# Four small edits to a tuned attention-plus-MLP kernel: epsilon inside bn_stats, a last tile in three pieces, a short final wait, and 1/den spread by DMAs

## The chip, the cores and the metric

The kernel runs on one core of one Trainium2 chip. The metric is the device time of one execution in microseconds (us). Runs are fast: the granted TensorE clock (the share of full speed that the profile shows as allowed) was 0.99 to 1.00.

Engine names as in the profile: PE is TensorE's matmuls, PEld its weight loads, DVE is VectorE, ACT is ScalarE, POOL is GpSimd, SP is SyncE, SPq its DMA queue. The pitch of a row of instructions is the time from one start to the next. A DMA lands when its semaphore reports it done.

## The reference

A layernorm without gain, then two branches on it, added to x. S = 2048 tokens, D = 640, F = 1536, 32 heads of 20, bf16.

```python
xn = (x - mean(x)) / sqrt(var(x) + 1e-5)
q, k, v = split_heads(xn @ wqkv)
phi = lambda t: where(t > 0, t + 1, exp(t)) + 1e-6
kv  = einsum("bhsd,bhse->bhde", phi(k), v)
z   = einsum("bhsd->bhd", phi(k))
den = einsum("bhqd,bhd->bhq", phi(q), z)[..., None] + 1e-6
a   = merge_heads(einsum("bhqd,bhde->bhqe", phi(q), kv) / den) @ wo
b   = gelu_tanh(xn @ w1 + b1) @ w2 + b2
return x + a + b
```

## The kernel before

The tokens are 16 tiles of 128 and 4 chunks of 512. The order on PE is: warm-up matmuls, transposes of the normalised tiles and the first MLP matmul (HG), the k projection, the sums over tokens, the q projection in chunks with the small matmuls that build one 640x640 matrix `Msb` of the attention between them, and last the output tiles. An output tile is 17 accumulating steps in PSUM, the memory that the matmuls write to: 12 of HG with W2, and 5 of PQ with Msb, where PQ is phi(q) times 1/den. Its eviction is the DVE instruction that adds x and writes the sum to SBUF, from where it is stored.

A small planner in the kernel records which instruction reads and writes which resource, and puts a semaphore wait wherever one depends on another, on the same engine too (PE excepted).

The layernorm statistics: `bn_stats` leaves sums over half a tile, `bn_aggr` makes mean and variance of the two halves, and `rstd` is the variance plus epsilon to the power of -1/2. Both halves of a tile's `stats` are one resource. `g` is POOL, `v` is DVE.

```python
def ln_half(t, h):
    s = t % 4
    Pl.ins(v, lambda e: e.bn_stats(stats[:, s, 6*h:6*h+6], x_in[:, t, h*HW:(h+1)*HW]),
           reads=[r_x[t]], writes=[r_stats[s]])

def ln_aggr(t):
    s = t % 4
    Pl.ins(v, lambda e: e.bn_aggr(aggr[:, s, :], stats[:, s, :]), reads=[r_stats[s]], writes=[r_aggr[s]])
    Pl.ins(g, lambda e: e.tensor_single_scalar(veps[:, s:s+1], aggr[:, s, 1:2], EPS, ALU.add), ...)
    Pl.ins(g, lambda e: e.tensor_tensor(out=rstd[:, s:s+1], in0=veps[:, s:s+1], in1=mhalf[:], op=ALU.pow), ...)

def ln_next(t):            # the order on DVE from tile 2 on
    if t + 1 < NT: ln_half(t + 1, 0); ln_half(t + 1, 1)
    ln_norm(t)
    if t + 1 < NT: ln_aggr(t + 1)
```

1/den of a chunk lies on 32 partitions, one for each head. A matmul with a 0/1 matrix `E4` spreads it to 128, ACT copies it to SBUF, DVE multiplies five tiles of PQ.

```python
def rden_step(c, b):
    # ... cut: cc is the columns of chunk c, rs a buffer in ek
    Pl.ins("tensor", lambda e: e.matmul(bank(b), E4[:, c, :], rden[:], start=True, stop=True), ...)
    Pl.ins("scalar", lambda e: e.activation(rs, bank(b), ACT.Copy), ...)
    for j in range(DT):
        Pl.ins(v, lambda e, j=j: e.tensor_tensor(out=PQ[:, j, cc], in0=PQ[:, j, cc], in1=rs, op=ALU.mult), ...)

def x_again(c):            # x is loaded once more for the residual, over the space of xnT
    # ... cut
    Pl.ins("sync", lambda e: e.dma_start(x_res[:, c*CH:(c+1)*CH, :], src), writes=[r_xr[c]] + r_xnT, dma=True)
```

The last tile is two halves of 320 columns, each with its own eviction and store, and at the end SP waits for every DMA it ever issued:

```python
def out_last(t):
    # ... cut
    for h in range(2):
        # ... cut
        Pl.ins("tensor", [mm(b, t, i, h) for i in range(JT + DT)], ...)
        Pl.ins(v, lambda e, h=h, hs=hs: e.tensor_tensor(out=out_sb[:, h, 0:HW], in0=bank(b+h, 0, HW), in1=x_res[:, t, hs], op=ALU.add), ...)
        Pl.ins("sync", lambda e, h=h, hs=hs: e.dma_start(ov[t*P:(t+1)*P, hs], out_sb[:, h, 0:HW]), ...)
# ... cut ...
for (waits, fns, ev, dma) in list(Pl.records["sync"]):
    if dma and ev is not None:
        Pl.wait_event("sync", ev)
```

Of the kernel before, what the change touches and what calls it, by code (L numbers as in the profile page):

```python
# [5 lines left out]
ALU = AluOpType  # L6
ACT = mybir.ActivationFunctionType
P = 128
FP32 = mybir.dt.float32
# [103 lines left out]
def bass_parallel_sum__linear_attn_block__dense_activation_gelu__prompt_kernel(  # L113
    nc: bass.Bass, A_x, A_wqkv, A_wo, B_x, B_w1, B_b1, B_w2, B_b2, out):
    Batch, S, D = A_x.shape
# [4 lines left out]
    CW = CH * P  # L120
    NC = NT // CH
    DT = D // P
    JT = F // P
    H = 32
    DH = D // H
    HW = D // 2
    assert DH == 4 * DT
    EPS = 1e-5

    Pl = Planner(nc)  # L130
    R_ = Pl.res
# [5 lines left out]
    with contextlib.ExitStack() as es:  # L137
        sb = lambda *a, **k: es.enter_context(nc.sbuf_tensor(*a, **k))
# [7 lines left out]
        x_res = xnTf[:].rearrange("p (t d) -> p t d", t=NT)  # L146
        PQ = sb("PQ", [P, DT, S], BF16)
        HG = sb("HG", [P, JT, S], BF16)
# [5 lines left out]
        W2 = sb("W2", [P, JT, D], BF16)  # L154
        Wo = sb("Wo", [P, DT, D], BF16)
        Mf = sb("Msb", [P, DT * D], BF16)
        Msb = Mf[:].rearrange("p (k d) -> p k d", k=DT)
# [11 lines left out]
        warm = sb("warm", [P, 512], BF16)  # L169
        stats = sb("stats", [P, 4, 12], FP32)  # L170
        aggr = sb("aggr", [P, 4, 2], FP32)
        veps = sb("veps", [P, 4], FP32)
        rstd = sb("rstd", [P, 4], FP32)
        mhalf = sb("mhalf", [P, 1], FP32)
        z_sb = sb("z_sb", [P, DT], FP32)
        ek = sb("ek", [P, 3, D], BF16)
        den_sb = sb("den_sb", [P, CW], FP32)
        rden = sb("rden", [P, CW], BF16)
        out_sb = sb("out_sb", [P, 2, D], BF16)

        ps = es.enter_context(nc.psum_tensor("ps", [P, 8 * 512], FP32))
        B_ = [R_("bank%d" % i) for i in range(8)]
        ring = [0]

        def take(n):
            b = ring[0]
            if n == 2 and b % 2:
                b += 1
            b %= 8
            ring[0] = (b + n) % 8  # L190
            return b

        def bank(b, lo=0, hi=512):
            return ps[:, b * 512 + lo: b * 512 + hi]
# [4 lines left out]
        def halves(ap):  # L199
            return ap.rearrange("p (a n) -> p a n", a=2)  # L200

        r_x = [R_("x%d" % t) for t in range(NT)]
        r_xr = [R_("xr%d" % c) for c in range(NC)]
        r_xb = [R_("xb%d" % t) for t in range(NT)]
        r_xn = [R_("xn%d" % t) for t in range(NT)]
        r_xnT = [R_("xnT%d" % t) for t in range(NT)]
# [2 lines left out]
        r_Wq, r_Wk, r_Wv, r_W2, r_Wo = R_("Wq"), R_("Wk"), R_("Wv"), R_("W2"), R_("Wo")  # L209
        r_b1tmp, r_b1c, r_b2 = R_("b1tmp"), R_("b1c"), R_("b2")  # L210
        r_ident, r_small, r_masks, r_bmask, r_E4, r_warm = R_("ident"), R_("small"), R_("masks"), R_("bmask"), R_("E4"), R_("warm")
        r_stats = [R_("stats%d" % i) for i in range(4)]
        r_aggr = [R_("aggr%d" % i) for i in range(4)]
        r_veps = [R_("veps%d" % i) for i in range(4)]
        r_rstd = [R_("rstd%d" % i) for i in range(4)]
        r_ek = [R_("ek%d" % i) for i in range(3)]
        r_PK = [R_("PK%d" % t) for t in range(NT)]
        r_PQ = [[R_("PQ%d_%d" % (c, j)) for j in range(DT)] for c in range(NC)]
# [5 lines left out]
        r_den, r_rden = R_("den"), R_("rden")  # L224
        r_out = [R_("out0"), R_("out1")]

        xv = A_x.rearrange("b s d -> (b s) d")
        ov = out.rearrange("b s d -> (b s) d")
# [25 lines left out]
        for c in range(2, NC):  # L254
# [9 lines left out]
        g = "gpsimd"  # L264
        v = "vector"
# [7 lines left out]
               reads=[r_ident], writes=[r_ident])  # L273
# [37 lines left out]
        def ln_half(t, h):  # L311
            s = t % 4
            Pl.ins(v, lambda e: e.bn_stats(stats[:, s, 6 * h:6 * h + 6], x_in[:, t, h * HW:(h + 1) * HW]),  # L313
                   reads=[r_x[t]], writes=[r_stats[s]])

        def ln_aggr(t):
            s = t % 4
            Pl.ins(v, lambda e: e.bn_aggr(aggr[:, s, :], stats[:, s, :]),
                   reads=[r_stats[s]], writes=[r_aggr[s]])
            Pl.ins(g, lambda e: e.tensor_single_scalar(veps[:, s:s + 1], aggr[:, s, 1:2], EPS, ALU.add),  # L320
                   reads=[r_aggr[s]], writes=[r_veps[s]])
            Pl.ins(g, lambda e: e.tensor_tensor(out=rstd[:, s:s + 1], in0=veps[:, s:s + 1],
                                                in1=mhalf[:], op=ALU.pow),
                   reads=[r_veps[s], r_small], writes=[r_rstd[s]])

        def ln_stats(t):
            ln_half(t, 0)
# [54 lines left out]
        def h_first(jbs):  # L382
# [7 lines left out]
            for jb, b in zip(jbs, bs):  # L390
# [6 lines left out]
               reads=[r_warm], writes=[r_b1c])  # L397
# [47 lines left out]
        for t in range(TD, NT):  # L445
            if t > TD:
                ln_next(t)
            Pl.ins("sync", lambda e, t=t: e.dma_start_transpose(xnT[:, :, t * P:(t + 1) * P], xn_tm[:, t, :]),
                   reads=[r_xn[t]], writes=[r_xnT[t]], dma=True)
# [22 lines left out]
        for t in range(NT):  # L472
            b = take(2)
            fns = []
# [10 lines left out]
        for f in range(DT):  # L485
            b = take(2)
            for t in range(NT):
# [3 lines left out]
                    reads=[r_xn[t], r_PK[t]], writes=B_[b:b + 2])  # L491
            Pl.ins("scalar", lambda e, b=b, f=f: e.activation(halves(GTb[:, f, :]), pair(b), ACT.Copy),
                   reads=B_[b:b + 2], writes=[r_GT[f]] + r_W1)

        Pl.ins(v, lambda e: e.tensor_tensor(out=zsum, in0=PK[:, 0, :], in1=PK[:, 1, :], op=ALU.add),
               reads=[r_PK[0], r_PK[1]], writes=[r_zsum])
        for t in range(2, NT):
            Pl.ins(v, lambda e, t=t: e.tensor_tensor(out=zsum, in0=zsum, in1=PK[:, t, :], op=ALU.add),  # L498
                   reads=[r_PK[t], r_zsum], writes=[r_zsum])
# [3 lines left out]
               reads=[r_zsum, r_zhl], writes=[r_zhl])  # L503
# [50 lines left out]
        def den_step():  # L554
# [8 lines left out]

            return b

        def rden_step(c, b):
            cc = slice(c * CW, (c + 1) * CW)
            s = c % 3
            rs = ek[:, s, 0:CW]
            Pl.ins("tensor", lambda e: e.matmul(bank(b), E4[:, c, :], rden[:], start=True, stop=True),  # L570
                   reads=[r_E4, r_rden], writes=[B_[b]])
            Pl.ins("scalar", lambda e: e.activation(rs, bank(b), ACT.Copy), reads=[B_[b]], writes=[r_ek[s]])  # L572
            for j in range(DT):
                Pl.ins(v, lambda e, j=j: e.tensor_tensor(out=PQ[:, j, cc], in0=PQ[:, j, cc], in1=rs, op=ALU.mult),  # L574
                       reads=[r_ek[s], r_PQ[c][j]], writes=[r_PQ[c][j]])

        def x_again(c):
            src = xv[c * CW:(c + 1) * CW, :].rearrange("(t p) d -> p t d", p=P)
            Pl.ins("sync", lambda e: e.dma_start(x_res[:, c * CH:(c + 1) * CH, :], src),
                   writes=[r_xr[c]] + r_xnT, dma=True)  # L580

        def xb(t):
            Pl.ins(v, lambda e: e.tensor_tensor(out=x_res[:, t, :], in0=x_res[:, t, :], in1=b2bc[:], op=ALU.add),
# [9 lines left out]
        for c in range(NC):  # L593
            x_again(c)


        def mm(b, t, i, h):
            tok = slice(t * P, (t + 1) * P)
            l, r = ((HG[:, i, tok], W2[:, i, :]) if i < JT else (PQ[:, i - JT, tok], Msb[:, i - JT, :]))
            return lambda e: e.matmul(bank(b + h, 0, HW), l, r[:, h * HW:(h + 1) * HW],  # L600
                                      start=(i == 0), stop=(i == JT + DT - 1))

        def mm_reads(t, i):
            return [r_HG[t][i], r_W2] if i < JT else [r_PQ[t // CH][i - JT], r_M[i - JT]]

        def out_w2(t, lo=0, hi=JT, b=None):
            b = take(2) if b is None else b
            for i in range(lo, hi):
                Pl.ins("tensor", [mm(b, t, i, 0), mm(b, t, i, 1)], reads=mm_reads(t, i), writes=B_[b:b + 2],
                       mark=(i == JT - 1))  # L610
            return b

        def out_fin(t, b):
            s = t % 2
            for i in range(JT, JT + DT):
                Pl.ins("tensor", [mm(b, t, i, 0), mm(b, t, i, 1)], reads=mm_reads(t, i), writes=B_[b:b + 2],
                       mark=(i == JT + DT - 1))
            xb(t)
            Pl.ins(v, lambda e: e.tensor_tensor(out=halves(out_sb[:, s, :]), in0=pair(b),  # L619
                                                in1=halves(x_res[:, t, :]), op=ALU.add),  # L620
                   reads=B_[b:b + 2] + [r_xb[t]], writes=[r_out[s]])
            Pl.ins("sync", lambda e: e.dma_start(ov[t * P:(t + 1) * P, :], out_sb[:, s, :]),
                   reads=[r_out[s]], dma=True)

        def out_last(t):
            b = take(2)
            xb(t)
            for h in range(2):
                hs = slice(h * HW, (h + 1) * HW)
                Pl.ins("tensor", [mm(b, t, i, h) for i in range(JT + DT)],  # L630
                       reads=[r for i in range(JT + DT) for r in mm_reads(t, i)], writes=[B_[b + h]])
                Pl.ins(v, lambda e, h=h, hs=hs: e.tensor_tensor(
                    out=out_sb[:, h, 0:HW], in0=bank(b + h, 0, HW), in1=x_res[:, t, hs], op=ALU.add),
                    reads=[B_[b + h], r_xb[t]], writes=[r_out[h]])
                Pl.ins("sync", lambda e, h=h, hs=hs: e.dma_start(ov[t * P:(t + 1) * P, hs], out_sb[:, h, 0:HW]),
                       reads=[r_out[h]], dma=True)

        bs = [out_w2(0)]
        db = den_step()
        bs += [out_w2(1), out_w2(2, 0, JT // 2)]  # L640
        rden_step(0, db)
        out_w2(2, JT // 2, JT, bs[2])
        for t in range(3):
            out_fin(t, bs[t])
        for t in range(3, NT - 1):
            b = out_w2(t)
            if t in (3, 6, 10):
                rden_step({3: 1, 6: 2, 10: 3}[t], take(1))
            out_fin(t, b)
        out_last(NT - 1)  # L650

        for (waits, fns, ev, dma) in list(Pl.records["sync"]):
            if dma and ev is not None:
                Pl.wait_event("sync", ev)

        with contextlib.ExitStack() as ses:
            for e_ in ENGINES:
# [33 lines left out]
```

## Time and profile before

| | before |
|---|---|
| time, median of 3 runs | 211.89 us (211.79 to 212.27) |
| span of the profiled run | 210.7 us (its time was 212.41 us, above all of the others) |
| PE busy | 98% |
| PE without work | to 5.8 us (but for warm-up), 0.5 us before 8.48, 0.2 us before 12.32, about 1 us in 122 to 126, after 207.8 |

From the page of the kernel before: the span, the busy time of each engine (us, share, instructions), and the chain of work that ended last, by engine.

```profile
span 210.7 us, 3883 instructions
PE 205.5 (98%) x1585; PEld 140.1 (67%) x1585; DVE 110.5 (52%) x226; ACT 76.8 (36%) x145; POOL 20.5 (10%) x61
...
PE 86%; DVE 7%; DMA 4%; SPq 1%; issue 1%; DVEq 0%
```

Only what shortens PE's own work, its few pauses, or the tail can move the time. The start, from the timelines of PE and of DVE: start, duration, line, operation, tiles and count, and in brackets the idle time before and what ended it.

```profile
8.48 3.78 PE L356 MATMUL ps<-xnT,W 128*128 128x128 bf16 x55 [0.35 <-DMA W<-in_B_w_dram]
12.32 0.45 PE L340 MATMUL ps<-ident,xn_tm 128*128 128x128 bf16 x5
```

```profile
10.88 1.02 DVE L313 BATCH_NORM_STATS2 stats<-xPK 128x6 f32<-128x320 bf16 x2 [0.69 <-DMA xPK<-in_A_x_dram]
11.82 0.43 DVE L333 TENSOR_SCALAR xn_tm<-xPK,aggr,rstd 128x640 bf16<-128x640 bf16 x1
```

PE waits first for a piece of W1 (it is loaded in four, 0 to 3) that lands at 8.43 us, then at 12.32 us for the transposes of tile 2. Tile 2 is normalised at 11.82 us, because DVE runs the two `bn_stats` of tile 3 first, and tile 3 lands at 10.86 us.

One of the three matmuls that the change takes out, in the timeline of PE. The next group starts 0.21 us later with nothing idle between, though the profile gives the matmul itself 0.38 us (matmuls overlap):

```profile
146.96 3.42 PE L600 MATMUL ps<-W,HG 128*128 128x320 bf16 x24
150.22 0.38 PE L570 MATMUL ps<-rden,E 128*128 128x512 bf16 x1
150.43 1.52 PE L600 MATMUL ps<-Msb,PQ 128*128 128x320 bf16 x10
```

The tail, from the timeline of all engines: the last eviction, and the two last stores merged into one row (the second is issued at 208.4 us). Then, from the answers about single lines of the program, the times from issue to landing of these two stores, and SP's final waits with their durations in ns and the start of the first and of the last.

```profile
206.50 2.19 SPq L635 DMA_DIRECT2D out_dram<-out_sb  x2
...
207.84 0.49 DVE L632 TENSOR_TENSOR out_sb<-ps,xnT 128x320 bf16<-128x320 f32 x1 [1.37 <-PE ps L600]
```

```profile
DMA to landing us min/median/max: 1.6/1.6/1.6
...
L108 SPq EVENT_SEMAPHORE  x17: 28/28/28, 208.7 to 210.2; - x17
```

The last store lands at 209.94 us, but the list of waits runs on to 210.2 us and the span ends at 210.66. Each instruction of the list carries two waits.

### The profile page before, as it was taken

Reading aid. Unit: us, or ns where it says so; the run is one execution under the profiler, and the core shown is the slowest. Engines: PE = TensorE matmul, PEld = TensorE weight load, DVE = VectorE, ACT = ScalarE, POOL = GpSimd, SP = SyncE. Lnnn points to the kernel's source line nnn. Section 1 sums busy time; section 2 is a strip of 40 time slices with the busy share of each in tenths; the row PEclk is TensorE's granted clock in tenths of the full one; section 3 lists DMA queues with packets and bytes.
Section 4 is the critical chain, followed back from the end, with each engine's and each line's share of the span. In section 5 each row is a group of like instructions: output and inputs, shape, how many; then the busy total and the mean of one; then the engine's idle time right before and its main releaser. Section 6 shows DMA issues by size and latency. Waiting matters only on the chain.

```text
span 210.7 us, 3883 instructions
## 1 busy us (share of the span) xinstructions
PE 205.5 (98%) x1585; PEld 140.1 (67%) x1585; DVE 110.5 (52%) x226; ACT 76.8 (36%) x145; POOL 20.5 (10%) x61
## 2 busy tenths in 40 slices
PE   7999999999999999999999999999999999999994
PEld 2689987444457777777666555677777777777772
DVE  4689981000008888999078866468451522263221
ACT  2579887666676554111253575110100100100000
POOL 2244557700000000000000000000000000000000
PEclk9999999999999999999999999999999999999999
DMA  5994758999000000000000000355411010001011
GB/s 165 340 349 99 101 111 101 347 321 346 10 0 0 0 3 0 0 3 0 0 0 3 0 5 0 124 138 170 163 35 54 9 65 31 31 31 34 31 62 33
DMA packets 21787, 17.46 MB, mean 83 GB/s; under 512 B 8713, under 2 KB 21769, under 8 KB 21769
## 3 DMA queue, kind: packets, MB, share of 16 engines
q1 hardware_dynamic: 21088, 16.72, 27.6%
q10 hardware_dynamic: 680, 0.49, 0.9%
q8 instruction: 12, 0.20, 0.4%
q14 instruction: 7, 0.05, 0.1%
HBM read 12.62 MB, written 2.62 MB: 72 GB/s over the span
## 4 chain that ended last, share of the span: by engine, by line
PE 86%; DVE 7%; DMA 4%; SPq 1%; issue 1%; DVEq 0%
PE ps L600 35%; PE ps L356 23%; PE ps L477 10%; PE ps L488 10%; PE ps L510 5%; DMA xPK<-in_A_x_dram 4%; DVE PQ L467 3%; DVE ek L465 1%; DVE W L534 1%; SPq L232 1%; PE ps L530 1%; PE ps L546 1%; DVE ZB L524 1%; PE ps L556 1%; DVE stats L313 0%
## 5 line engine op out<-in xcount | busy, mean ns | idle before, releaser
L600 PE MATMUL ps<-W,HG 128*128 128x320 bf16 x384 | 54.9, 299 | 0.0
L356 PE MATMUL ps<-xnT,W 128*128 128x128 bf16 (+2 forms) x435 | 52.0, 282 | 0.4 <-DMA W<-in_B_w_dram 0.4
L600 PEld LDWEIGHTS ps<-W,HG 128*128 128x128 bf16 x384 | 37.5, 98 | 15.2 <-issue 0.4
L356 PEld LDWEIGHTS ps<-xnT,W 128*128 128x128 bf16 x435 | 35.5, 98 | 16.1 <-DMA W<-in_B_w_dram 0.5
L360 ACT ACTIVATE HG<-ps,b1c 128x128 bf16<-128x128 f32 (+2 forms) x87 | 40.0, 492 | 13.2 <-PE ps L356 11.1
L465 DVE TENSOR_SCALAR ek<-ek 128x512 bf16<-128x512 bf16 (+1 forms) x36 | 10.9, 304 | 40.2 <-ACT ek L464 39.1
L464 ACT ACTIVATE ek<-ps 128x512 bf16<-128x512 f32 (+1 forms) x36 | 23.2, 644 | 20.4 <-PE ps L510 11.2
L619 DVE TENSOR_TENSOR out_sb<-ps,xnT 128x640 bf16<-128x640 f32 x15 | 12.4, 825 | 29.3 <-PE ps L600 26.2
L600 PE MATMUL ps<-Msb,PQ 128*128 128x320 bf16 x160 | 24.2, 299 | 0.0
L510 PE MATMUL ps<-xnT,Wqkv 128*128 128x512 bf16 x100 | 22.1, 379 | 0.0
L477 PE MATMUL ps<-Wqkv,xnT 128*128 128x320 bf16 x160 | 21.9, 299 | 0.0
L488 PE MATMUL ps<-xPK,xn_tm 128*128 128x320 bf16 x160 | 21.9, 299 | 0.0
L572 ACT ACTIVATE ek<-ps 128x512 bf16<-128x512 f32 x4 | 2.4, 597 | 49.2 <-PE ps L570 49.2
L600 PEld LDWEIGHTS ps<-Msb,PQ 128*128 128x128 bf16 x160 | 15.6, 98 | 6.3
L477 PEld LDWEIGHTS ps<-Wqkv,xnT 128*128 128x128 bf16 x160 | 15.7, 98 | 6.2
L488 PEld LDWEIGHTS ps<-xPK,xn_tm 128*128 128x128 bf16 x160 | 15.7, 98 | 6.1
L510 PEld LDWEIGHTS ps<-xnT,Wqkv 128*128 128x128 bf16 x100 | 11.6, 118 | 9.5 <-issue 0.2
L313 DVE BATCH_NORM_STATS2 stats<-xPK 128x6 f32<-128x320 bf16 x32 | 15.2, 475 | 3.5 <-DMA xPK<-in_A_x_dram 2.9
L467 DVE SCALAR_TENSOR_TENSOR PQ<-ps,ek 128x512 bf16<-128x512 f32 x20 | 13.8, 692 | 2.1
L467 DVE SCALAR_TENSOR_TENSOR xPK<-ps,ek 128x640 bf16<-128x640 f32 x16 | 13.2, 825 | 1.7
L498 DVE TENSOR_TENSOR Msb<-Msb,xPK 128x640 f32<-128x640 f32 x14 | 11.6, 825 | 0.5
L574 DVE TENSOR_TENSOR PQ<-PQ,ek 128x512 bf16<-128x512 bf16 x20 | 7.1, 419 | 9.0 <-ACT ek L572 9.0
(64 smaller groups left out, 89.3 us busy)
## 6 DMA issues: line engine op xcount, KB each, us to landing
xnT<-in_A_x_dram SPq DMA_DIRECT2D x4, 640.0 KB, 4.1
Wqkv<-in_A_wqkv_dram SPq DMA_DIRECT2D x3, 800.0 KB, 6.9
out_dram<-out_sb SPq DMA_DIRECT2D x15, 160.0 KB, 1.8
W<-in_B_w_dram SPq DMA_DIRECT2D x1, 1920.0 KB, 15.3
W<-in_B_w_dram SPq DMA_DIRECT2D x3, 480.0 KB, 7.6
xPK<-in_A_x_dram SPq DMA_DIRECT2D x2, 640.0 KB, 9.3
Wo<-in_A_wo_dram SPq DMA_DIRECT2D x1, 800.0 KB, 10.5
xPK<-in_A_x_dram SPq DMA_DIRECT2D x4, 160.0 KB, 4.5
```

Source lines behind the costliest of these rows:

```text
L313: Pl.ins(v, lambda e: e.bn_stats(stats[:, s, 6 * h:6 * h + 6], x_in[:, t, h * HW:(h + 1) * HW]), reads=[r_x[t]], writes=[r_stats[s]])
L356: Pl.ins("tensor", [(lambda e, k=k: e.matmul(bank(b, 0, w), W1[:, k, jb * P:(jb + 1) * P], xnT[:, k, tok], start=(k == 0), stop=(k == DT - ...
L360: Pl.ins("scalar", lambda e: e.activation(HG[:, jb, tok], bank(b, 0, w), ACT.Gelu_apprx_tanh, bias=b1c[:, jb:jb + 1]), reads=[B_[b], r_b1c ...
L464: Pl.ins("scalar", lambda e: e.activation(e2, src, ACT.Exp), reads=br, writes=[r_ek[s]])
L465: Pl.ins(v, lambda e: e.tensor_scalar(et, et, 1.0, 1e-6, ALU.min, ALU.add), reads=[r_ek[s]], writes=[r_ek[s]])
L467: Pl.ins(v, lambda e: e.scalar_tensor_tensor(out=d2, in0=src, scalar=0.0, in1=e2, op0=ALU.max, op1=ALU.add), reads=br + [r_ek[s]], writes= ...
L477: fns.append(lambda e, k=k, h=h, b=b, t=t: e.matmul(bank(b + h, 0, HW), xnT[:, k, t * P:(t + 1) * P], Wqkv[:, k, D + h * HW:D + (h + 1) * ...
L488: Pl.ins("tensor", [(lambda e, t=t, h=h, b=b, f=f: e.matmul(bank(b + h, 0, HW), xn_tm[:, t, f * P:(f + 1) * P], PK[:, t, h * HW:(h + 1) * ...
L498: Pl.ins(v, lambda e, t=t: e.tensor_tensor(out=zsum, in0=zsum, in1=PK[:, t, :], op=ALU.add), reads=[r_PK[t], r_zsum], writes=[r_zsum])
L510: Pl.ins("tensor", [(lambda e, k=k, j=j, b=b: e.matmul(bank(b), Wqkv[:, k, j:D:DT], xnT[:, k, cc], start=(k == 0), stop=(k == DT - 1))) fo ...
L600: return lambda e: e.matmul(bank(b + h, 0, HW), l, r[:, h * HW:(h + 1) * HW], start=(i == 0), stop=(i == JT + DT - 1))
L619: Pl.ins(v, lambda e: e.tensor_tensor(out=halves(out_sb[:, s, :]), in0=pair(b), in1=halves(x_res[:, t, :]), op=ALU.add), reads=B_[b:b + 2] ...
```

## The change

Four parts, meant to take work off PE and off the two ends of the kernel: (1) 1/den of chunks 1 to 3 is spread by four small DMAs each instead of a matmul and an ACT copy, and the reloads of x no longer wait for each other; (2) the last tile is three pieces of 320, 192 and 128 columns; (3) SP's final wait is for the last 3 stores; (4) epsilon, times D, is added to a sum that `bn_stats` leaves, while DVE does the second half, instead of to the variance afterwards, and for this the halves of `stats` became two resources. The diff, cut:

```diff
 def ln_half(t, h):
-           reads=[r_x[t]], writes=[r_stats[s]])
+           reads=[r_x[t]], writes=[r_stats[s][h]])
+    if h == 0:
+        Pl.ins(g, lambda e: e.tensor_single_scalar(stats[:, s, 2:3], stats[:, s, 2:3], D * EPS, ALU.add),
+               reads=[r_stats[s][0]], writes=[r_stats[s][0]])
 def ln_aggr(t):
-           reads=[r_stats[s]], writes=[r_aggr[s]])
-    Pl.ins(g, lambda e: e.tensor_single_scalar(veps[:, s:s + 1], aggr[:, s, 1:2], EPS, ALU.add), ...)
-    Pl.ins(g, lambda e: e.tensor_tensor(out=rstd[:, s:s + 1], in0=veps[:, s:s + 1], ...
+           reads=r_stats[s], writes=[r_aggr[s]])
+    Pl.ins(g, lambda e: e.tensor_tensor(out=rstd[:, s:s + 1], in0=aggr[:, s, 1:2], ...
 ... (cut)
+def rden_dma(c):
+    for i in range(4):
+        Pl.ins("sync", lambda e, i=i: e.dma_start(rdb(c)[i:P:4, :], rden[H * c:H * (c + 1), :]),
+               reads=[r_rden], writes=[r_rdb[c][i]] + ([r_rdb[0][i]] if c == 3 else []), dma=True)
 def x_again(c):
-           writes=[r_xr[c]] + r_xnT, dma=True)
+           writes=[r_xr[c]] + (r_xnT if c == 0 else []), dma=True)
 ... (cut)
 def out_last(t):
-    for h in range(2):
+    for i, w in enumerate((HW, 3 * 64, P)):      # matmuls, eviction and store for each piece
 ... (cut)
+rden_dma(1)
 for t in range(3, NT - 1):
     b = out_w2(t)
     if t in (3, 6, 10):
-        rden_step({3: 1, 6: 2, 10: 3}[t], take(1))
+        rden_scale({3: 1, 6: 2, 10: 3}[t])
     out_fin(t, b)
+    if t in (3, 7):
+        rden_dma({3: 2, 7: 3}[t])
 out_last(NT - 1)
-for (waits, fns, ev, dma) in list(Pl.records["sync"]):
-    if dma and ev is not None:
-        Pl.wait_event("sync", ev)
+for (waits, fns, ev, dma) in Pl.records["sync"][-3:]:
+    Pl.wait_event("sync", ev)
```

More of the change, by code (lines that the diff above doesn't have):

```diff
@@ L171, in bass_parallel_sum__linear_attn_block__dense_activation_gelu__prompt_kernel @@
         aggr = sb("aggr", [P, 4, 2], FP32)
-        veps = sb("veps", [P, 4], FP32)
         rstd = sb("rstd", [P, 4], FP32)
@@ L211, in bass_parallel_sum__linear_attn_block__dense_activation_gelu__prompt_kernel @@
         r_ident, r_small, r_masks, r_bmask, r_E4, r_warm = R_("ident"), R_("small"), R_("masks"), R_("bmask"), R_("E4"), R_("warm")
-        r_stats = [R_("stats%d" % i) for i in range(4)]
+        r_stats = [[R_("stats%d_%d" % (i, h)) for h in range(2)] for i in range(4)]
         r_aggr = [R_("aggr%d" % i) for i in range(4)]
-        r_veps = [R_("veps%d" % i) for i in range(4)]
         r_rstd = [R_("rstd%d" % i) for i in range(4)]
@@ L318, in ln_aggr @@
             Pl.ins(v, lambda e: e.bn_aggr(aggr[:, s, :], stats[:, s, :]),
-                   reads=[r_stats[s]], writes=[r_aggr[s]])
-            Pl.ins(g, lambda e: e.tensor_single_scalar(veps[:, s:s + 1], aggr[:, s, 1:2], EPS, ALU.add),
-                   reads=[r_aggr[s]], writes=[r_veps[s]])
-            Pl.ins(g, lambda e: e.tensor_tensor(out=rstd[:, s:s + 1], in0=veps[:, s:s + 1],
+                   reads=r_stats[s], writes=[r_aggr[s]])
+            Pl.ins(g, lambda e: e.tensor_tensor(out=rstd[:, s:s + 1], in0=aggr[:, s, 1:2],
                                                 in1=mhalf[:], op=ALU.pow),
-                   reads=[r_veps[s], r_small], writes=[r_rstd[s]])
+                   reads=[r_aggr[s], r_small], writes=[r_rstd[s]])
         def ln_stats(t):
@@ L564, in den_step, with rden_scale, rdb @@
             return b
+        def rden_scale(c):
+            cc = slice(c * CW, (c + 1) * CW)
+            for j in range(DT):
+                Pl.ins(v, lambda e, j=j: e.tensor_tensor(out=PQ[:, j, cc], in0=PQ[:, j, cc], in1=rdb(c), op=ALU.mult),
+                       reads=r_rdb[c] + [r_PQ[c][j]], writes=[r_PQ[c][j]])
+        ekf = ek[:].rearrange("p a d -> p (a d)")
+        r_rdb = [[R_("rdb%d_%d" % (c, i)) for i in range(4)] for c in range(NC)]
+        def rdb(c):
+            return ekf[:, c % 3 * CW:(c % 3 + 1) * CW]
         def rden_step(c, b):
-            cc = slice(c * CW, (c + 1) * CW)
-            s = c % 3
-            rs = ek[:, s, 0:CW]
             Pl.ins("tensor", lambda e: e.matmul(bank(b), E4[:, c, :], rden[:], start=True, stop=True),
                    reads=[r_E4, r_rden], writes=[B_[b]])
-            Pl.ins("scalar", lambda e: e.activation(rs, bank(b), ACT.Copy), reads=[B_[b]], writes=[r_ek[s]])
-            for j in range(DT):
-                Pl.ins(v, lambda e, j=j: e.tensor_tensor(out=PQ[:, j, cc], in0=PQ[:, j, cc], in1=rs, op=ALU.mult),
-                       reads=[r_ek[s], r_PQ[c][j]], writes=[r_PQ[c][j]])
+            Pl.ins("scalar", lambda e: e.activation(rdb(c), bank(b), ACT.Copy), reads=[B_[b]],
+                   writes=r_rdb[c] + r_ek)
+            rden_scale(c)
+        def rden_dma(c):
+            for i in range(4):
+                Pl.ins("sync", lambda e, i=i: e.dma_start(rdb(c)[i:P:4, :], rden[H * c:H * (c + 1), :]),
+                       reads=[r_rden], writes=[r_rdb[c][i]] + ([r_rdb[0][i]] if c == 3 else []), dma=True)
         def x_again(c):
@@ L594, in bass_parallel_sum__linear_attn_block__dense_activation_gelu__prompt_kernel, with mm_ops @@
             x_again(c)
+        r_out3 = R_("out3")
+        def mm_ops(t, i):
+            tok = slice(t * P, (t + 1) * P)
+            return ((HG[:, i, tok], W2[:, i, :]) if i < JT else (PQ[:, i - JT, tok], Msb[:, i - JT, :]))
         def mm(b, t, i, h):
-            tok = slice(t * P, (t + 1) * P)
-            l, r = ((HG[:, i, tok], W2[:, i, :]) if i < JT else (PQ[:, i - JT, tok], Msb[:, i - JT, :]))
+            l, r = mm_ops(t, i)
             return lambda e: e.matmul(bank(b + h, 0, HW), l, r[:, h * HW:(h + 1) * HW],
@@ L625, in out_last @@
         def out_last(t):
-            b = take(2)
             xb(t)
-            for h in range(2):
-                hs = slice(h * HW, (h + 1) * HW)
-                Pl.ins("tensor", [mm(b, t, i, h) for i in range(JT + DT)],
-                       reads=[r for i in range(JT + DT) for r in mm_reads(t, i)], writes=[B_[b + h]])
-                Pl.ins(v, lambda e, h=h, hs=hs: e.tensor_tensor(
-                    out=out_sb[:, h, 0:HW], in0=bank(b + h, 0, HW), in1=x_res[:, t, hs], op=ALU.add),
-                    reads=[B_[b + h], r_xb[t]], writes=[r_out[h]])
-                Pl.ins("sync", lambda e, h=h, hs=hs: e.dma_start(ov[t * P:(t + 1) * P, hs], out_sb[:, h, 0:HW]),
-                       reads=[r_out[h]], dma=True)
+            lo = 0
+            for i, w in enumerate((HW, 3 * 64, P)):
+                b = take(1)
+                o = out_sb[:, (0, 1, 0)[i], (0, 0, HW)[i]:(0, 0, HW)[i] + w]
+                hs = slice(lo, lo + w)
+                lo += w
+                fns = []
+                for q in range(JT + DT):
+                    l, r = mm_ops(t, q)
+                    fns.append(lambda e, l=l, r=r, q=q, b=b, hs=hs, w=w: e.matmul(
+                        bank(b, 0, w), l, r[:, hs], start=(q == 0), stop=(q == JT + DT - 1)))
+                Pl.ins("tensor", fns, reads=[r for q in range(JT + DT) for r in mm_reads(t, q)], writes=[B_[b]])
+                Pl.ins(v, lambda e, b=b, hs=hs, w=w, o=o: e.tensor_tensor(
+                    out=o, in0=bank(b, 0, w), in1=x_res[:, t, hs], op=ALU.add),
+                    reads=[B_[b], r_xb[t]], writes=[r_out3 if i == 2 else r_out[i]])
+                Pl.ins("sync", lambda e, hs=hs, o=o: e.dma_start(ov[t * P:(t + 1) * P, hs], o),
+                       reads=[r_out3 if i == 2 else r_out[i]], dma=True)
         bs = [out_w2(0)]
```

## The prediction

> **What bounds the kernel now.** TensorE: the page shows PE busy 98% of the 210.7 us span at a granted clock of 0.999, and the chain of waits is 86% PE. The PE timeline pauses before 5.8 us (warm-up), 0.5 us before 8.48 us (a W1 load), 0.2 us before 12.32 us (normalisation of tile 2, behind bn_stats of an x load that lands at 10.86 us), about 1 us at 122 to 126 us (DVE phi work), and after 207.8 us. From 126 to 207.8 us it never stops.
>
> **The four parts, costed.**
>
> 1. *1/den by DMA.* Three of four 128x512 matmuls (rden,E) leave PE; each takes 0.216 us to the next start (PE timeline), in a stretch without a gap: -0.65 us. The ACT copies (0.60 us) are off the path. The DMAs must land before the multiplies that tiles 4, 8, 12 need, at about 155, 174 and 192 us; rden is ready at 140.3 us, so there is slack. The x reloads (4.1 us each) no longer wait for each other; they leave together at about 132 us and are needed one by one from 143 us. I expect no PE wait.
>
> 2. *Last tile in pieces 320, 192, 128.* PE pitch is 136 ns at 320 columns and 56 ns at 128 (timeline), so about 82 ns at 192: 17x(136+82+56) = 4.66 us against 34x136 = 4.62, +0.03. The Trainium skill, "TensorE: Matmul & The Clock Gate", section "Back-to-back issue gap", gives a sustained 81 ns at 128 columns and calls 56 the isolated gap; this trace has 56 in a stream of weight-load and matmul pairs, and I use it. The last eviction shrinks: 0.49 us at 320 columns and 0.30 at 140 (groups by form) give about 0.29 at 128, -0.20. The last store is 32 KB, not 80: stores of 160 and 80 KB landed after 1.8 and 1.6 us, so about 1.5, -0.1.
>
> 3. *Final wait on three stores.* SyncE runs 17 wait instructions from 208.7 to 210.2 us, some 60 ns apart, after issuing the last store at 208.4; that store landed at about 209.95. So the list ends about 0.25 us after it could: -0.25.
>
> 4. *Epsilon in bn_stats.* Takes a 0.22 us GpSimd instruction out of each rstd chain, but PE's early gates are loads and the bn_stats after them, and rstd of tile 2 is ready (11.1 us) before DVE reaches it (11.8). For tile 1 the addition queues behind the first pow (0.57 us) and may hold bn_aggr 0.05 to 0.1 us; the 0.5 us wait on W1 hides that. Later tiles gain 0.1 us each on DVE, off the path. 0.
>
> Sum: -0.65 +0.03 -0.30 -0.25 = -1.2 us (0.5%).
>
> **Predicted:** 210.7 us, range 210.1 to 211.4. Faster by over 2%: 1%; within 2%: 98%; slower by over 2%: 1%.
>
> **Right or wrong in the profile.** One rden,E matmul; no new PE wait from 126 us on; last matmul about 0.6 us earlier; last eviction near 0.29 us; one to three final waits, the span ending about 0.45 us after the last landing instead of 0.7; PE's first gates within 0.1 us of 8.48 and 12.32.
>
> **What would make it wrong.** Loads landing at other times by chance (0.2 to 0.4 us either way); rden DMAs queued behind 2.6 MB of x so late that PE waits at tile 4; 256-byte rows slowing the last store; SyncE's waits not being what ends the span.

## The result, and the profile after

| | before | after |
|---|---|---|
| median, 4 runs each | 211.98 us | 210.73 us (210.39 to 210.95) |
| ratio | | 0.9938, 95% interval 0.992 to 0.9956 |
| span of the profiled run | 210.7 us | 209.0 us |
| time of the profiled run | 212.41 us | 210.68 us |

A ratio is the mean time of one kernel's fast runs over that of the other's of the same rounds, so not quite the ratio of the medians. 0.9938 of 212 us is 1.3 us less, with 0.9 to 1.7 in the interval.

From the page of the changed kernel, the same lines as before:

```profile
span 209.0 us, 3950 instructions
PE 204.9 (98%) x1599; PEld 141.0 (67%) x1599; DVE 108.8 (52%) x227; ACT 75.1 (36%) x142; POOL 20.2 (10%) x61
...
PE 92%; DVE 6%; issue 1%; DVEq 0%
```

The chain has no DMA in it now. From the end of the chain in order of time (start, duration, what), the output tiles run without a pause behind the one spreading matmul that is left:

```profile
140.64 0.22 PE ps L578
140.86 61.12 PE ps L617 x450
201.98 4.67 PE ps L653 x51
206.66 0.02 issue
206.68 0.29 DVE out_sb L656
```

The start, from the timelines of PE and DVE:

```profile
8.17 3.77 PE L355 MATMUL ps<-xnT,W 128*128 128x128 bf16 x55
11.78 0.44 PE L339 MATMUL ps<-ident,xn_tm 128*128 128x128 bf16 x5
```

```profile
10.29 0.89 DVE L311 BATCH_NORM_STATS2 stats<-xPK 128x6 f32<-128x320 bf16 x2 [0.32 <-DMA xPK<-in_A_x_dram]
11.09 0.43 DVE L332 TENSOR_SCALAR xn_tm<-xPK,aggr,rstd 128x640 bf16<-128x640 bf16 x1
```

The tail: the row of the three stores, the last eviction, their times from issue to landing, and SP's final waits (one instruction with two; the branch after it carries the third).

```profile
205.30 2.03 SPq L659 DMA_DIRECT2D out_dram<-out_sb  x3
...
206.68 0.29 DVE L656 TENSOR_TENSOR out_sb<-ps,xnT 128x128 bf16<-128x128 f32 x1 [0.59 <-PE ps L653]
```

```profile
DMA to landing us min/median/max: 1.5/1.5/1.6
...
L108 SPq EVENT_SEMAPHORE  x1: 28/28/28, 208.5 to 208.5; - x1
```

The profiled spans differ by 1.70 us, more than the 1.3 us of the times: the profiled run of before was a long one, that of the change an ordinary one. Cut at three points of the trace, the difference falls apart (times in us):

| stretch | before | after | difference |
|---|---|---|---|
| start to the transposes of tile 2 | 12.316 | 11.777 | -0.54 |
| from there to the first W,HG matmul | 119.270 | 119.252 | -0.02 |
| to the start of the last eviction | 76.256 | 75.652 | -0.60 |
| last eviction to the end | 2.817 | 2.274 | -0.54 |

The last two rows are -1.15 us; the prediction had added up -1.2. The first row was not predicted: at the start I had expected no change.

### The profile page after: what moved, and what is told of

It reads as the page before. It is cut to its first block, busy times and chain, and to the rows that moved or that the text cites. A ratio compares the mean times of both kernels' runs of the same rounds, so it can differ in the third digit from the quotient of the medians.

```text
span 209.0 us, 3950 instructions
## 1 busy us (share of the span) xinstructions
PE 204.9 (98%) x1599; PEld 141.0 (67%) x1599; DVE 108.8 (52%) x227; ACT 75.1 (36%) x142; POOL 20.2 (10%) x61
## 4 chain that ended last, share of the span: by engine, by line
PE 92%; DVE 6%; issue 1%; DVEq 0%
PE ps L617 33%; PE ps L355 25%; PE ps L487 10%; PE ps L476 10%; PE ps L509 5%; DVE PQ L466 3%; PE ps L298 2%; PE ps L653 2%; DVE ek L464 1%; DVE W L533 1%; PE ps L529 1%; PE ps L545 1%; DVE ZB L523 1%; PE ps L555 1%; PE ps L385 1%
## 5 line engine op out<-in xcount | busy, mean ns | idle before, releaser
L617 PE MATMUL ps<-W,HG 128*128 128x320 bf16 x360 | 51.4, 299 | 0.0
L617 PEld LDWEIGHTS ps<-W,HG 128*128 128x128 bf16 x360 | 35.1, 98 | 14.2 <-issue 0.4
L617 PE MATMUL ps<-Msb,PQ 128*128 128x320 bf16 x150 | 22.5, 299 | 0.0
L617 PEld LDWEIGHTS ps<-Msb,PQ 128*128 128x128 bf16 x150 | 14.6, 98 | 5.7
L311 DVE BATCH_NORM_STATS2 stats<-xPK 128x6 f32<-128x320 bf16 x32 | 13.6, 466 | 2.3 <-DMA xPK<-in_A_x_dram 2.3
L491 ACT ACTIVATE W<-ps 128x640 bf16<-128x640 f32 x5 | 3.5, 704 | 18.2 <-PE ps L487 14.6
L321 POOL TENSOR_TENSOR rstd<-aggr,mhalf 128x1 f32<-128x1 f32 x16 | 9.1, 568 | 8.9 <-DVE aggr L319 8.9
```

Source lines behind the costliest of these rows:

```text
L311: Pl.ins(v, lambda e: e.bn_stats(stats[:, s, 6 * h:6 * h + 6], x_in[:, t, h * HW:(h + 1) * HW]), reads=[r_x[t]], writes=[r_stats[s][h]])
L617: return lambda e: e.matmul(bank(b + h, 0, HW), l, r[:, h * HW:(h + 1) * HW], start=(i == 0), stop=(i == JT + DT - 1))
```

## The experiments

Two theories for the -0.54 us at the start. **L**: it is chance. The loads are unchanged but land at other times in each run; part 4 gains nothing. **E**: part 4 gains it. For the rest, the theory to test is that parts 1 to 3 are worth -0.65, -0.27 and -0.25 us.

All twelve runs of the experiments gave correct results. Since the start scatters, I read each profile twice: the time to the transposes of tile 2 (the start), and the stretch from there to the end, which repeats within about 0.02 us between profiles of kernels that do the same work there.

| kernel | what it is | ratio to before (95%) | start | stretch to end |
|---|---|---|---|---|
| before | | | 12.32 | 198.34 |
| p_den | part 1 alone | 0.9959 (0.9943 to 0.9975) | 11.59 | 197.70 |
| p_tail | part 2 alone | 0.9989 (0.9974 to 1.0005) | 12.18 | 198.22 |
| p_wait | part 3 alone | 0.9982 (0.9967 to 0.9997) | 12.17 | 198.10 |
| p_eps | part 4 alone | 0.9994 (0.9974 to 1.0014) | 11.94 | 198.35 |
| p_split | of part 4 the two resources alone | 0.9982 (0.9947 to 1.0017) | 11.69 | 198.34 |
| a_noeps | the change without part 4 | 0.9943 (0.9916 to 0.997) | 11.88 | 197.19 |
| after | the change | 0.9938 (0.992 to 0.9956) | 11.78 | 197.18 |
| a_same | the change again | 0.9931 (0.9897 to 0.9966) | 11.82 | 197.17 |
| a_xser | the change, x reloads one after the other | 0.9937 (0.9899 to 0.9975) | 11.97 | 197.18 |
| a_m | the change, Msb matmuls moved | 0.9888 (0.9862 to 0.9913) | 12.10 | 196.38 |
| a_m_r | a_m again | 0.99 (0.9855 to 0.9944) | 12.55 | 196.37 |
| a_m0 | a_m, chunk 0 by DMA, with a fault | 0.9916 (0.9889 to 0.9942) | 11.60 | 196.91 |
| a_m1 | a_m, chunk 0 by DMA, mended | 0.9903 (0.9864 to 0.9941) | 12.11 | 196.14 |

p_den, p_tail, p_wait and p_eps shared one chip and the runs of before on it; p_split, a_noeps, a_m and a_m0 did so too; and so did a_same, a_xser, a_m1 and a_m_r. In the second group one of eleven runs of before took 213.82 us, in the last one of nine 213.91 us, both at a clock of 0.992. They widen the intervals, and without them the ratios of these groups would be about 0.001 higher.

### Part 1 alone (p_den)

```diff
 for t in range(3, NT - 1):
-        rden_step({3: 1, 6: 2, 10: 3}[t], take(1))
+        rden_scale({3: 1, 6: 2, 10: 3}[t])
 # with rden_dma, and the x reloads freed of each other; out_last, the final waits and the layernorm as before
```

> Part 1 alone (1/den of chunks 1 to 3 by DMA, x reloads not waiting for each other). Sum theory: three matmuls at a pitch of 0.216 us leave a gapless stretch, so -0.65 us (ratio about 0.997), no PE wait from 126 us on, and from the start of the first W,HG matmul to the last matmul 0.65 us less. Rival (the DMAs disturb PE or DVE, or the ACT and DVE work taken off was on the path): a change of under 0.3 us or over 1 us in that stretch.

Measured: the stretch is 0.64 us shorter, and from the first W,HG matmul to the start of the last matmul it went from 75.920 to 75.273, -0.647 us, which is three times 0.216. The time fell by 0.87 us (0.5 to 1.2 in the interval). The profiled run also had the earliest start of all, 11.59 us, without part 4: x tile 3 landed at 10.14 us instead of 10.86.

### Part 2 alone (p_tail)

```diff
 def out_last(t):
-    for h in range(2):
+    for i, w in enumerate((HW, 3 * 64, P)):
 # the rest as before
```

> Part 2 alone (last tile in 320, 192, 128). Sum theory: PE time of the last tile +0.03 us, last eviction 0.49 to 0.29 us, last store lands 1.5 instead of 1.6 us after its issue, so the last landing is about 0.3 us earlier; but the list of 17 final waits is now what ends the span, since it runs some 1.5 us from the last issue whatever the store does: -0.2 us in time. Rival (tail parts simply add): -0.3 us.

Measured: from the last eviction's start to the last landing 1.755 us instead of 2.100, and PE's part 0.04 us longer. But of the 0.30 us that this makes, the stretch keeps 0.13 (0.2 was expected); in time, -0.2 us with -0.55 to +0.1 in the interval tells nothing. SP's waits in this kernel, from the answer about their line:

```profile
L108 SPq EVENT_SEMAPHORE  x18: 17/28/28, 208.5 to 209.9; - x18
```

The last store landed at 209.51 us, and the list ran to 209.9: it takes 1.5 us from its first wait, here as before, whatever the store does, so here it alone ends the span (0.88 us from landing to end, instead of 0.72). Parts 2 and 3 help each other.

### Part 3 alone (p_wait)

```diff
-for (waits, fns, ev, dma) in list(Pl.records["sync"]):
-    if dma and ev is not None:
-        Pl.wait_event("sync", ev)
+for (waits, fns, ev, dma) in Pl.records["sync"][-3:]:
+    Pl.wait_event("sync", ev)
```

> Part 3 alone (SyncE waits for the last 3 stores only). Sum theory: the end of the span moves from 0.7 to about 0.45 us after the last landing, -0.25 us. Rival (the waits hide behind the store): 0 within 0.1 us.

Measured: 0.456 us from the last landing to the end, instead of 0.717; the stretch is 0.24 us shorter. The rival (the waits hide behind the store) falls. The three parts alone add up to -1.01 us in the stretch, and together give -1.16: the missing 0.15 us is about what the wait list had swallowed of part 2 (0.16 us more from landing to end).

### Part 4 alone (p_eps), and its bookkeeping alone (p_split)

p_eps is the first two blocks of the diff above. p_split leaves the epsilon where it was:

```diff
-           reads=[r_x[t]], writes=[r_stats[s]])
+           reads=[r_x[t]], writes=[r_stats[s][h]])
-           reads=[r_stats[s]], writes=[r_aggr[s]])
+           reads=r_stats[s], writes=[r_aggr[s]])
```

> Part 4 alone (epsilon added to a bn_stats sum, the two halves of stats tracked apart). Theory L (load timing): nothing systematic at the start; PE's first W1 matmul after tile 1 and the transposes of tile 2 follow the landings of the loads, as before, and the time is the same within 0.15 us; the 0.55 us that the profile of the whole change shows at the start is mostly chance. Rival E (epsilon part matters): two bn_stats take 0.88 instead of 1.02 us in the profile, tile 2 is normalised 0.15 us or more earlier after its landing, and the time falls by 0.15 to 0.5 us.

> Of part 4 only the bookkeeping: the two halves of stats are two resources, so the second bn_stats no longer waits for the first; epsilon stays a GpSimd addition after bn_aggr. Theory W (the wait between the two bn_stats is what part 4 gains): the second bn_stats starts about 0.40 us after the first instead of 0.53, the tile-2 transposes follow the landing of x tile 3 by about 1.32 us instead of 1.45 where that landing gates them, the same as with the whole of part 4. Rival G (the GpSimd addition taken off the rstd chain is what gains): still 1.45 us. Time: the same as before within 0.25 us either way.

The timeline of DVE in p_eps, and then in p_split:

```profile
10.64 0.89 DVE L311 BATCH_NORM_STATS2 stats<-xPK 128x6 f32<-128x320 bf16 x2 [0.55 <-DMA xPK<-in_A_x_dram]
11.45 0.43 DVE L332 TENSOR_SCALAR xn_tm<-xPK,aggr,rstd 128x640 bf16<-128x640 bf16 x1
```

```profile
10.10 0.89 DVE L313 BATCH_NORM_STATS2 stats<-xPK 128x6 f32<-128x320 bf16 x2 [0.22 <-DMA xPK<-in_A_x_dram]
10.95 0.45 DVE L333 TENSOR_SCALAR xn_tm<-xPK,aggr,rstd 128x640 bf16<-128x640 bf16 x1
```

In p_eps the pair of `bn_stats` takes 0.89 us instead of 1.02: the second starts 0.410 us after the first instead of 0.529. Tile 2 is normalised 0.83 us after tile 3 has landed, instead of 0.96, and its transposes follow the landing by 1.314 us instead of 1.454. So part 4 does something: some 0.13 us, by removing a wait on DVE. In p_split the second `bn_stats` comes 0.411 us after the first as well, with the POOL addition still in its old place. So theory W holds for most of it: it is the bookkeeping. The rest of rival G stands in one small point: in p_split tile 3 landed so early (10.08 us) that `rstd` of tile 2 became the later one, and the normalisation came 0.87 us after the landing, not 0.83. That the transposes gain their 0.13 us by the bookkeeping alone was not seen there, since PE was held by another load in that run (below).

In time, p_eps is the same as before (-0.1 us, -0.55 to +0.3 in the interval); that alone just leaves room for half a us. What speaks against half a us is the trace, in which part 4 shortens the way from the landing by 0.13 us and no more. The part of theory L that said nothing is gained falls too.

### The change without part 4 (a_noeps), and the change again (a_same)

> The whole change with part 4 undone. Theory L (load timing made the start faster by chance): ratio to before as of the whole change within 0.15 us, 0.9935 to 0.9955; from the first W,HG matmul to the end of the span the same as with the whole change, 77.93 us, within 0.1. Rival E (part 4 gains half a us at the start): 0.4 us or more slower than the whole change, ratio 0.996 or more.

> The changed kernel again, on the same chip as the next three. Ratio to before 0.992 to 0.9955. In its profile: from the first W,HG matmul to the end 77.93 us within 0.1; the tile-2 transposes 1.32 us after the landing of x tile 3, or later only if PE itself or the W1 load is late.

The start of a_noeps came at 11.88 us, almost as early as with part 4, and 0.43 us earlier than in the profile of before. Its stretch is that of the change within 0.02 us. So a start about as early comes without part 4. By ratio a_noeps lies in the expected range, but time does not decide: its interval would not exclude rival E, and its mean of 211.11 us lies 0.34 us above that of a_same in the next group on the same chip, between what L and E expected, with single runs 1 us apart. One profile's start would not decide either; all of them together do.

What sets the start, then? The landings of three loads and the start of tile 2's transposes, in all profiles (us):

| kernel | W1 piece 0 | W1 piece 1 | x tile 3 | transposes of tile 2 | after piece 0 | after tile 3 |
|---|---|---|---|---|---|---|
| before | 6.30 | 8.43 | 10.86 | 12.32 | 6.02 | 1.45 |
| p_den | 6.48 | 7.76 | 10.14 | 11.59 | 5.11 | 1.45 |
| p_tail | 6.91 | 8.30 | 10.73 | 12.18 | 5.27 | 1.45 |
| p_wait | 7.00 | 8.29 | 10.72 | 12.17 | 5.17 | 1.45 |
| p_eps | 6.74 | 8.20 | 10.62 | 11.94 | 5.19 | 1.31 |
| a_m | 7.13 | 8.35 | 10.78 | 12.10 | 4.97 | 1.32 |
| a_m0 | 6.78 | 7.87 | 10.28 | 11.60 | 4.82 | 1.32 |
| a_m1 | 7.18 | 8.35 | 10.80 | 12.11 | 4.93 | 1.32 |
| p_split | 6.91 | 7.66 | 10.08 | 11.69 | 4.78 | 1.61 |
| a_noeps | 7.10 | 7.77 | 10.22 | 11.88 | 4.78 | 1.66 |
| a_same | 7.04 | 7.80 | 10.22 | 11.82 | 4.78 | 1.60 |
| a_xser | 7.19 | 8.00 | 10.43 | 11.97 | 4.78 | 1.54 |
| a_m_r | 7.77 | 8.02 | 10.45 | 12.55 | 4.78 | 2.10 |
| after | 6.68 | 7.82 | 10.26 | 11.78 | 5.10 | 1.51 |

There are two gates. In the first eight rows tile 3 is the later one, and the transposes come a fixed 1.45 us after it, or 1.31 to 1.32 with part 4. In the next five, piece 0 of W1 is, and they come 4.78 us after it, with or without part 4. The two race within a few tenths of a us, and they land at other times in each run: 6.30 to 7.77 us and 10.08 to 10.86. Part 4 gains 0.13 us where tile 3 is last by as much, and nothing where W1 is. (It needs tile 3 to be last by 0.13 us. In p_den it was last by 0.01 us only: the 55 matmuls before the transposes take 3.60 us at their pitch, and they began 3.61 us before.) Nor does part 4 show in the mean: the transposes came at 12.03 us in the five profiles with nothing of it, and at 11.98 us in the eight with all of it. This is PE in a_same, held at 7.09 us by W1 and then without a pause up to the transposes of tile 2:

```profile
7.09 1.01 PE L385 MATMUL ps<-xnT,W 128*128 128x128 bf16 x15 [0.21 <-DMA W<-in_B_w_dram]
7.94 0.44 PE L339 MATMUL ps<-ident,xn_tm 128*128 128x128 bf16 x5
8.22 3.77 PE L355 MATMUL ps<-xnT,W 128*128 128x128 bf16 x55
11.82 0.44 PE L339 MATMUL ps<-ident,xn_tm 128*128 128x128 bf16 x5
```

The profiled run of the change (last row) fits neither. There PE was late by itself (the chain of this profile lies on PE from 1.25 us to 110 us): its transposes of tile 0 followed each other at 80 to 107 ns up to 6.6 us, where in the profile of before they did so at 55 to 67 ns from 5.8 us on. The Trainium skill, "TensorE: Matmul & The Clock Gate", section "What you observe", gives 107 ns for a slow and 56 ns for a fast clock, and says that the point of change varies from run to run; these traces show both pitches, and a point of change that varies, from about 4.2 us of the span in a_noeps to 7.2 us in p_wait.

So theory L is right about the -0.54 us: the profile of before happened to have one of the late starts of its gate. Its run shows it too: it took 212.41 us, where the four timed runs of before took 211.79 to 212.27; that of the change took 210.68, in the middle of its four. Why the loads land when they do stays open. Theory L is wrong in that part 4 gains nothing.

### The reloads of x one after the other again (a_xser)

```diff
-           writes=[r_xr[c]] + (r_xnT if c == 0 else []), dma=True)
+           writes=[r_xr[c]] + r_xnT, dma=True)
```

> The whole change, but each reload of x waits for the one before it, as before. If the slack counted in the prediction is right: the first multiply by the spread 1/den of chunk 1 moves some 3 us later, PE waits nowhere, from the first W,HG matmul to the end 77.93 us within 0.1, time the same as the whole change within 0.2 us. Rival (the loosened reloads are part of the gain): 0.3 us or more slower.

Measured: same time, and the same stretch within 0.01 us. From the timeline of DVE in the change, and then in a_xser: the multiplies by 1/den of chunk 1.

```profile
147.40 1.75 DVE L568 TENSOR_TENSOR PQ<-PQ,ek 128x512 bf16<-128x512 bf16 x5
```

```profile
149.76 0.82 DVE L636 TENSOR_TENSOR out_sb<-ps,xnT 128x640 bf16<-128x640 f32 x1 [3.10 <-DMA out_dram<-out_sb]
150.50 1.76 DVE L568 TENSOR_TENSOR PQ<-PQ,ek 128x512 bf16<-128x512 bf16 x5
```

DVE waits 3.1 us for a store that was issued late behind the slow reloads, and the multiplies come 3.1 us later. PE does not notice: it needs them only at about 154 us. The slack that the prediction counted on is there, and the freed reloads gain no time here.

### A better version: the Msb matmuls later (a_m, a_m_r)

The largest pauses left on PE are around the matmuls that build `Msb`. From the timeline of PE in the change:

```profile
121.91 1.29 PE L545 MATMUL ps<-Wo,W 128*32 128x320 bf16 x32
123.38 0.75 PE L545 MATMUL ps<-Wo,W 128*32 128x320 bf16 x16 [0.18 <-DVE PQ L466]
124.38 1.29 PE L545 MATMUL ps<-Wo,W 128*32 128x320 bf16 x32 [0.24 <-DVE PQ L466]
```

They take PSUM banks in quick succession while DVE is still over 2 us behind with phi(q) of the chunk before. In a_m they come after the q projection of the last chunk, the W,HG matmuls of tile 0 and the den matmuls:

```diff
-        m_step()
         q_chunk(3)
 # ... cut: m_step and den_step now get their banks as arguments
-        bs = [out_w2(0)]
-        db = den_step()
-        bs += [out_w2(1), out_w2(2, 0, JT // 2)]
-        rden_step(0, db)
+        b0 = out_w2(0)
+        b1, b2, b3 = [(b0 + i) % 8 for i in (2, 4, 6)]
+        den_step(b1)
+        m_step([b2, b3, b1, b2, b3])
+        bs = [b0, out_w2(1, b=b1), out_w2(2, 0, JT // 2, b2)]
+        rden_step(0, b3)
         out_w2(2, JT // 2, JT, bs[2])
+        ring[0] = b3
```

> An attempt at a better version: the whole change, and the Msb matmuls moved behind the q projection of chunk 3, the W,HG matmuls of tile 0 and the den matmuls, so that DVE has caught up with phi before PE takes banks again. If the three waits of 0.34, 0.41 and 0.10 us around the Msb matmuls are what is left on PE from 7 to 206 us, then -0.7 to -0.9 us against the whole change: about 209.8, ratio to before 0.989 to 0.991. If the waits only move (to den, or to ACT copies of Msb), under 0.3 us.

> The better version without the DMA for chunk 0, on the same chip as the others: ratio to before 0.988 to 0.991; 0.8 us faster than the whole change, 0.2 us slower than the mended version. If the two are not told apart by time, the profile's stretch from the tile-2 transposes to the end decides.

From the timeline of PE in a_m, the same matmuls in one run, with no wait of note:

```profile
127.55 3.42 PE L615 MATMUL ps<-W,HG 128*128 128x320 bf16 x24
130.90 1.26 PE L554 MATMUL ps<-PQ,ZB 128*32 128x512 bf16 x20
131.99 3.07 PE L545 MATMUL ps<-Wo,W 128*32 128x320 bf16 x80
```

The stretch is 0.80 us shorter than the change's, in both profiles of it. In time, the change and a_m_r on one chip had means of 210.77 and 210.24 us, 0.54 us apart (0.8 was expected; the starts differ by as much as that).

### And chunk 0 by DMA (a_m0, a_m1)

```diff
+        rden_dma(0)
         rden_dma(1)
+        rden_scale(0)      # with the W,HG matmuls of tile 3 ahead of the first output tiles, no rden_step
 # rden_dma in a_m0:
-    writes=[r_rdb[c][i]] + ([r_rdb[0][i]] if c == 3 else []), dma=True)
+    writes=[r_rdb[c][i]] + ([r_rdb[0][i]] if c == 3 else r_ek if c == 0 else []), dma=True)
 # rden_dma in a_m1:
+    writes=[r_rdb[c][i]] + ([r_rdb[0][i]] if c == 3 else r_ek if (c, i) == (0, 0) else []), dma=True)
```

> The same with 1/den of chunk 0 by DMA too, and the W,HG matmuls of tile 3 ahead of the first out tiles to cover its latency: one more matmul of 0.216 us off PE, so -0.2 us against the version before it, about 209.6, ratio 0.988 to 0.990, if the four DMAs and the five multiplies are done by the time PE has run the W,HG matmuls of four tiles; if not, PE waits there and the gain turns into a loss.

> The better version with 1/den of chunk 0 by DMA, mended: in the try before it each of the four DMAs was made to wait for the one before by a resource listed four times (issues 1.7 us apart, last landing 144.3 us, PE waited 0.5 us at 144.9). Now they are issued within 3.5 us, land by about 141 us, and PE has no wait there: from the tile-2 transposes to the end about 196.2 us instead of 196.4 (without it) and 197.2 (the whole change); ratio to before 0.987 to 0.990.

a_m0 failed by my own fault: listing the old users of the buffer as written by each of the four DMAs made each wait for the one before. They left 1.7 us apart, the last landed at 144.29 us, and PE waited. From the timelines of DVE and PE in a_m0:

```profile
144.42 1.77 DVE L567 TENSOR_TENSOR PQ<-PQ,ek 128x512 bf16<-128x512 bf16 x5 [8.62 <-DMA ek<-rden]
```

```profile
144.90 5.86 PE L615 MATMUL ps<-Msb,PQ 128*128 128x320 bf16 x40 [0.34 <-DVE PQ L567]
```

In a_m1 they land in time. From its timelines of DVE and PE:

```profile
141.02 1.76 DVE L567 TENSOR_TENSOR PQ<-PQ,ek 128x512 bf16<-128x512 bf16 x5 [4.71 <-DMA ek<-rden]
```

```profile
135.12 9.95 PE L615 MATMUL ps<-W,HG 128*128 128x320 bf16 x72
144.91 2.34 PE L615 MATMUL ps<-Msb,PQ 128*128 128x320 bf16 x16
```

The stretch is 0.24 us shorter than a_m's, one matmul of 0.216 us and a little. The times (means 210.17 and 210.24 us on one chip) do not tell the two apart, and the ratio of a_m1 just missed the expected 0.987 to 0.990. The spans of these runs do differ, by 0.3 us (means 208.2 and 208.5), but the times of a_m0 and a_m1 lie 1.7 to 2.0 us above their spans, those of all other kernels 1.7 to 1.8: what the span gains the time does not show, and why is not known. Both beat the change (mean 210.77 us there); a_m1 has the shortest stretch, 196.14 us against 197.18 and 198.34 of before.

## Why the prediction was right

- **The time.** 210.7 was predicted, 210.73 measured. An agreement that close is luck, since single runs lie half a us apart and the starts add their own chance. The sum itself was right for its reasons: the stretch after the start shortened by 1.16 us, in the profile of the change and in two more of the same work, where the sum said 1.2.
- **1/den by DMA, -0.65.** p_den: -0.647. The pitch of a matmul in a gapless stretch, not its listed duration of 0.38 us, was the right price. No PE wait appeared; a_xser shows that there were 3 us to spare.
- **Last tile, +0.03 on PE and -0.30 after it.** Measured +0.04 and -0.345 (eviction start to landing). The last pieces ran at 82.5 and 56 ns a matmul. The section "Back-to-back issue gap" of the Trainium skill's "TensorE: Matmul & The Clock Gate" would have had 81 ns for 128 columns, by estimate 0.4 us more over 17 matmuls; the trace of before decided rightly.
- **The stores.** 160, 80 and 32 KB landed 1.8, 1.6 and 1.5 us after issue by SyncE. That most of it does not scale with size agrees with the Trainium skill, "DMA: Bandwidth & Descriptors", section "Anatomy of one DMA — SWDGE (gpsimd) path", which says it of DMAs issued by GpSimd.
- **Final wait, -0.25.** p_wait: -0.24 in the stretch, -0.26 from landing to end. What the prediction did not say is that parts 2 and 3 depend on each other: alone, part 2 would have kept 0.13 us only.
- **Epsilon, 0: mis-sized.** I priced the POOL instruction that leaves the `rstd` chain, rightly found it off the path, and overlooked that the same edit takes a DVE wait out between the two `bn_stats`, which is on the path. It gains 0.13 us where tile 3's landing gates PE, and 0 where W1's does (five of fourteen profiles). I also expected the later addition for tile 1 to hold `bn_aggr` by 0.05 to 0.1 us, and so it did, by 0.1: `bn_aggr` started 0.14 us after the second `bn_stats` had ended, instead of 0.03, but 0.09 us earlier than before, thanks to the faster `bn_stats`.
- **First gates within 0.1 us of 8.48 and 12.32: wrong.** They came at 8.17 and 11.78. The prediction had named landings by chance as its first risk, with 0.2 to 0.4 us; the tile-2 transposes ranged from 11.59 to 12.55 us over the fourteen profiles.

## What to carry to other kernels

Price a removed instruction by the distance to the next one's start on the engine that never pauses, and check with one stage's length in the trace, which repeats to 0.02 us, where run times scatter by half a us. Then check the time too: a_m1 gained in the span and not in the time. When a profile pair differs at the start, look at load landings over several runs before you credit the change. Declare dependencies as fine as the data is: one resource for two halves cost a wait of 0.12 us on DVE, and one listed four times turned four parallel DMAs into a chain.

## What the Trainium skill lacked or had wrong

- "TensorE: Matmul & The Clock Gate", section "Back-to-back issue gap": its sustained 81 ns at 128 columns and 131 ns at 512 were not seen. Streams of weight-load and matmul pairs ran at 56 ns (128), 82.5 (192), 136 (320) and 216 (512), which is what the page gives as the isolated gap, N/2.4 + 2.5 ns.
- Same page, section "What you observe": it puts the change to the fast clock at about 4 us into activity, give or take 0.5. Here the first warm-up matmul starts at 1.25 us. In a_noeps, p_split and a_m0 the 512-column warm-up matmuls went from a pitch of 427 to 216 ns at about 4.2 us, 2.9 to 3.0 us later. Pitches of 107 ns lasted to 6.6 us in the profile of the change and to 7.2 us in that of p_wait, 5.3 and 6 us later (with short pauses of PE between).
- "VectorE: DVE Perf Modes", section "The DRAIN you can't avoid": it measured, with eight `tensor_copy`, that a semaphore after each op costs nothing extra. Between two `bn_stats` of 320 columns, a wait of the second on the first cost 0.12 us: 0.529 us from start to start with it, 0.411 without. The same section does say that a next op that is not held starts earlier, but not by how much.
- "DMA: Bandwidth & Descriptors", section "Anatomy of one DMA — SWDGE (gpsimd) path": the fixed 2.0 us is fitted for DMAs issued by GpSimd, and the page has no such fit for SyncE's. Stores issued by SyncE landed 1.5 us (32 KB) to 1.8 us (160 KB) after issue, where nothing held them up.
- No page that I read prices a list of waits on SyncE: 17 wait instructions took 1.5 us, mostly 60 to 75 ns apart, with one gap of 0.48 us. The 25 of p_den took 1.5 us too, without such a gap; what the gap is stays open.
